# An attention-then-MLP kernel: the first rows of k are loaded in float32 by SyncE and rounded on chip

## The chip, the cores and the metric

The kernel runs on one core of one Trainium2 chip. The metric is the device time of one execution in microseconds (us), as the median of several runs; lower is better. Five engines work side by side and meet through semaphores: TensorE (PE, with its weight loads shown as PEld), VectorE (DVE), ScalarE (ACT), GpSimd (POOL) and SyncE (SP). Loads and stores are DMAs, which an engine issues from its own queue and which then run beside the engines.

## The reference

Two stages in a row, with float32 inputs and a float32 output:

- Attention over 8 batches, 8 heads, 576 positions and 64 channels a head. A query sees its own position and the 127 before it. Each head adds a linear bias: minus its slope (1/2, 1/4, ... 1/256) times the distance.
- The heads side by side make 4608 rows of 512. They go through `h = x @ w_in` (512 by 2048), an ELU, and `@ w_out` (2048 by 512).

```python
scores = scale * np.matmul(q, k.transpose(0, 1, 3, 2))
scores = np.where((rel >= 0) & (rel < 128), scores + bias[None], -1e9)
attn = softmax(scores);  x = attn @ v
h = x @ w_in
out = np.where(h > 0, h, np.exp(np.minimum(h, 0)) - 1) @ w_out
```

## The kernel before, in words

**Types and loads.** Everything on chip is float16, except sums and the output. The inputs are float32, so every load is a DMA issued by GpSimd, which converts on the way (L101 for the first two batches' q and k, L108 for later ones, L114 v, L119 w_in, L122 w_out). GpSimd issues them in the order of the code, one after another, between its other work. SyncE issues the stores of the output and the transposes of x of later batches; its first store is issued at 40.7 us.

**Batches 0 and 1** bring q and k with rows on partitions, and TensorE turns them by transposes (`turn_first`, L136) into PSUM. A copy by DVE or ACT (L140) then puts the turned pieces into `QT` and `KT`, with channels on partitions. `split` says how a batch's 576 rows are cut into parts: for part 0 of batch 0, 256 rows as 64 partitions with 4 rows each. So one half (four of eight heads) is 16 small transposes of 64x64. Later batches are turned by DVE (L145).

**Scores of batch 0** have the bias added by TensorE: `early_bias` (L183) multiplies `SI` (for each head an identity times the head's slope) by `RB` (the distances, with a large negative number outside the window), and `early_scores` (L191) adds q times k into the same PSUM bank. `early_expo` (L197, L200) is the exponential on ACT. From batch 1 on the exponential of the plain score is multiplied by a table `TAB` instead (`first_weigh`, `weigh`); `TAB[:, 0]` is made by eight exponentials on ACT (L464), `TAB[:, 1]` by two copies on DVE (L473, L474). `values` (L253 to L260) multiplies by v and divides on DVE, `turn` (L289, L290) turns the result into `xT`.

**The MLP** takes rows of `xT` as they come: `hidden` (L305) multiplies by w_in, ACT and GpSimd make the exponential side of the ELU into `e` (L312 to L316), `elu` (L323, DVE) puts both sides together into `g`, and `output` and `product` (L329, L393) multiply by w_out.

**The order** is written out by hand. What an engine gets first in the code it does first. The start (L428 to L488) is a plain list: a memset for the warming matmuls, GpSimd's loads and memsets, DVE's chain from the iota of positions (L432) through the identity (L454), the distances (L455 to L457) and `SI` (L460), ACT's eight exponentials, 22 matmuls on ones (`warm`, L424) that keep TensorE busy, then batch 0's first turns, biases, scores and values:

```python
load_first(0, 1, 0)                      # k, 256 rows
nc.gpsimd.iota(rel, pattern=[[1, 256]], base=0, channel_multiplier=-1)
load_first(0, 0, 0)                      # q, 256 rows
load_v(0, 0)
load_v(0, 1)
load_wi(0)
```

After it comes a plan of numbered slots, each with one step of `hidden`. `at(s, f, ...)` puts a piece of work into slot s; in a slot come first the pieces of `before`, then `hidden`, then the `elu` of the slot before (`done`; in slots 1, 4 and 5 it stands elsewhere), then the pieces of `at` in the order of the code, then outputs. In the profile slot 0 begins on TensorE at 13.01 us, slot 3 at 20.66, slot 4 at 22.42.

**Buffers the change touches.** `T` are four tiles of 128 x 2048 float16, filled with sums of w_out's blocks from slot 11 on; until then `fore[1]` to `fore[4]` are the same memory used for other things (`far`, `RB`, `SI`, `rel`, `wz`). `fore[2]` is not used early. `st` is a ring of two buffers for the q and k of batches from 2 on. `hp`, `op`, `av`, `sp` are PSUM banks.

Of the kernel before, what the change touches and what calls it, by code (L numbers as in the profile page):

```python
# [7 lines left out]
F32 = mybir.dt.float32  # L8
F16 = mybir.dt.float16
I32 = mybir.dt.int32  # L10
AF = mybir.ActivationFunctionType
# [7 lines left out]
def kernel(  # L19
# [9 lines left out]
    nc = tc.nc  # L29
    B, H, S, D = q.shape  # L30
# [6 lines left out]
    R = S // 64  # L37
    V = nc.vector

    const = ctx.enter_context(tc.tile_pool(name="const", bufs=1))  # L40
    stage = ctx.enter_context(tc.tile_pool(name="stage", bufs=2))
# [7 lines left out]
    def one(shape, dt, name):  # L49
        return const.tile(shape, dt, name=name, tag=name)  # L50
# [6 lines left out]
    fore = [t.rearrange("p j c -> p (j c)") if t is not None else None for t in T]  # L57
    RB = fore[3][:, 1024:1536]
# [3 lines left out]
    TAB = one([128, 2, 4, 2, 256], F16, "TAB")  # L62
# [14 lines left out]
    sp = [spa[:, 0, :], spa[:, 1, :]] + [ps_s.tile([128, 512], F32, name=f"sp{i}", tag=f"sp{i}") for i in (2, 3)]  # L77
    hp = [ps_h.tile([128, 512], F32, name=f"hp{i}", tag=f"hp{i}") for i in range(2)]
    av = ps_v.tile([128, 512], F32, name="av", tag="av")
    op = ps_o.tile([128, 512], F32, name="op", tag="op")  # L80
    AB = sp[0:2]
# [3 lines left out]
    st = {}  # L85
    s0 = gpool.tile([128, NFC * 512], F16, name="s0", tag="g")
    s1 = one([128, 2 * H * 6 * D], F16, "s1")
    s0 = [t[:, 0:2 * H * 6 * D].rearrange("p (w h j d) -> p w h j d", w=2, h=H, j=6) for t in (s0, s1)]

    def split(b, w, part):  # L90

        if b == 0 and w == 1:
            return ((0, 64, 4, 0, 0), (64, 64, 5, 256, 0))[part]
        if b == 0:
            return ((0, 64, 4, 0, 0), (64, 64, 2, 256, 0), (64, 64, 3, 384, 2))[part]
        return ((0, 128, 4, 0, 0), (0, 64, 1, 512, 4))[part]

    def load_first(b, w, part):

        p0, n, m, r0, j0 = split(b, w, part)  # L100
        nc.gpsimd.dma_start(  # L101
            s0[b][p0:p0 + n, w, :, j0:j0 + m, :].rearrange("p h j d -> p h (j d)"),
            (q, k)[w][b, :, r0:r0 + n * m, :].rearrange("h (p j) d -> p h (j d)", j=m))

    def load_qk(b, w, g):
        if b not in st:
            st[b] = stage.tile([128, 2, 2, R, 2, D], F16, name="st")
        nc.gpsimd.dma_start(  # L108
            st[b][32 * g:32 * g + 32, w, :, :, :, :].rearrange("p h n j d -> p (h n) (j d)"),
            (q, k)[w][b, 2 * g:2 * g + 2, :, :].rearrange("h (n i j) d -> i (h n) (j d)", i=32, j=2))  # L110
# [16 lines left out]
    def turn_first(b, w, part, half, bank, copy):  # L127

        p0, n, m, r0, j0 = split(b, w, part)
        nh = 4 if n * m < 256 else 2  # L130
        t = bank.bitcast(F16)[:, 0:nh * m * n].rearrange("p (x j r) -> p x j r", x=nh, j=m)
        r = slice(p0, p0 + n)
        for x in range(nh):
            for j in range(m):
                for hh in range(2):
                    nc.tensor.transpose(t[64 * hh:64 * hh + 64, x, j, :], s0[b][r, w, 4 * hh + nh * half + x, j0 + j, :],  # L136
                                        ident[r, r])
        t = t.rearrange("p x j r -> p x r j")
        o = (Q0, K0)[w][b][:, nh * half:nh * half + nh, r0:r0 + m * n]
        copy(o.rearrange("p x (r j) -> p x r j", j=m), t)  # L140
# [8 lines left out]
    with tc.manual_schedule():  # L149
# [29 lines left out]
        def early_bias(banks, c0):  # L179

            for x in range(4):
                for hh in range(2):
                    nc.tensor.matmul(banks[hh][:, 128 * x:128 * x + 128], SI[:, 4 * hh + x, :], RB[:, c0:c0 + 128],  # L183
                                     start=x == 0, stop=False, skip_group_check=True)

        def early_scores(banks, u, c0):
            k0, q0 = 128 * u, 128 * u + c0
            for x in range(4):
                for hh in range(2):
                    r = slice(64 * hh, 64 * hh + 64)  # L190
                    nc.tensor.matmul(banks[hh][:, 128 * x:128 * x + 128], kt_[0][r, x * S + k0:x * S + k0 + 128],  # L191
                                     Q0[0][r, x, q0:q0 + 128], start=False, stop=True, skip_group_check=True)
# [50 lines left out]
        def values(b, i, part, bank=av):  # L243

            m = 128 if i < 4 else 64
            banks = (part, part + 2) if b < 2 else (2 * part, 2 * part + 1)
            parts = [(3, 128, 3), (3, 192, 4)] if i == 4 else [(i, 0, i)] + ([(i - 1, 128, i - 1)] if i else [])
            a = bank[:, 0:4 * (D + 1)].rearrange("p (x h d) -> p x h d", x=2, h=2)
            for x, g in enumerate(banks):
                for h2 in range(2):  # L250
                    for j, (u, c, n) in enumerate(parts):
                        c += 512 * g + 256 * h2
                        nc.tensor.matmul(a[:, x, h2, :], ex_[u][:, c:c + 128], VP[b % 2][:, n, 2 * g + h2, 0:D + 1],  # L253
                                         start=j == 0, stop=j == len(parts) - 1)
            if part == 0:
                xnt[b, i] = work.tile([128, 4, 2, D], F16, name="xn", tag="xn", bufs=4)
            o = xnt[b, i][0:m, part::2, :, :] if b < 2 else xnt[b, i][0:m, 2 * part:2 * part + 2, :, :]
            r = work.tile([128, 2, 2], F32, name="rden", tag="rden", bufs=2)
            V.reciprocal(out=r[0:m], in_=a[0:m, :, :, D])
            V.tensor_tensor(out=o, in0=a[0:m, :, :, 0:D], in1=r[0:m].unsqueeze(3).broadcast_to([m, 2, 2, D]),  # L260
                            op=ALU.mult)
# [18 lines left out]
        def turn(b, i, copy=None, bank=op):  # L280
            n = 128 if i < 4 else 64
            o = (b * S + 128 * i) % RING
            x = xnt.pop((b, i)).rearrange("p g h d -> p (g h d)")
            if copy is None:
                nc.sync.dma_start_transpose(out=xT[:, :, o:o + n], in_=x[0:n, :])
                return
            t = bank.bitcast(F16)[:, 0:512].rearrange("p (c r) -> p c r", c=4)
            for c in range(4):
                nc.tensor.transpose(t[:, c, 0:n], x[0:n, 128 * c:128 * c + 128], ident[0:n, 0:n])  # L289
            copy(xT[:, :, o:o + n], t[:, :, 0:n])  # L290
# [131 lines left out]
        def warm(n, bank=op):  # L422
            for _ in range(n):
                nc.tensor.matmul(bank[:, 0:256], wz[:, 0:128], wz, start=True, stop=True)  # L424
# [3 lines left out]
        rel = fore[3][:, 1536:2048].bitcast(I32)  # L428
        far = fore[1][:, 0:256]
        V.memset(wz, 1.0)  # L430
        load_first(0, 1, 0)
        nc.gpsimd.iota(rel, pattern=[[1, 256]], base=0, channel_multiplier=-1)  # L432
        load_first(0, 0, 0)
        load_v(0, 0)
        load_v(0, 1)
        load_wi(0)
        load_first(0, 0, 1)
        load_first(0, 1, 1)
        load_first(0, 0, 2)
# [18 lines left out]
        slope = [2.0 ** (-8.0 * (h + 1) / H) for h in range(H)]  # L458
# [1 line left out]
            V.tensor_scalar(out=SI[:, h, :], in0=ident, scalar1=8.0 * slope[h], scalar2=None, op0=ALU.mult)  # L460
        V.memset(VP[0][:, :, :, D:D + 1], 1.0)

        for h in range(H):
            nc.scalar.activation(TAB[:, 0, h // 2, h % 2, :], RB[:, 0:256], AF.Exp, scale=slope[h])  # L464
        warm(22)
        turn_first(0, 1, 0, 0, hp[0], V.tensor_copy)
        turn_first(0, 1, 0, 1, op, V.tensor_copy)
        early_bias(AB, 0)
        turn_first(0, 0, 0, 0, hp[1], nc.scalar.copy)
        turn_first(0, 0, 0, 1, av, V.tensor_copy)  # L470
        V.tensor_copy(RB[:, 256:448], RB[:, 0:192])
        V.tensor_copy(RB[:, 448:512], RB[:, 0:64])
        V.tensor_copy(TAB[:, 1, :, :, 0:192], TAB[:, 0, :, :, 0:192])  # L473
        V.tensor_copy(TAB[:, 1, :, :, 192:256], TAB[:, 0, :, :, 0:64])  # L474
        early_bias(sp[2:4], 128)
        early_scores(AB, 0, 0)
        early_expo(AB, 0, 0)
        early_scores(sp[2:4], 0, 128)
# [5 lines left out]
        values(0, 0, 1, op)  # L484
        warm(5, sp[0])
        turn(0, 0, V.tensor_copy, hp[0])
        values(0, 1, 0)
        values(0, 1, 1, op)  # L488

# [3 lines left out]
        def at(s, f, *a):  # L493
            tasks.setdefault(s, []).append((f, a))
# [29 lines left out]
        for o in range(16 * NTB):  # L524
            t, ts, f = o // 16, o // 4 % 4, o % 4
# [32 lines left out]
        at(5, first_scores, 0, 3, 1, 0)  # L558
        at(5, first_expo, 0, 3, 1, 0, 0, 256)
        at(5, done, 4)  # L560
        at(9, values, 0, 3, 0)
        at(9, values, 0, 3, 1, sp[3])
        at(10, values, 0, 4, 0)
# [35 lines left out]
        for b in range(2, B):  # L599
            for u in range(4):  # L600
                a = START[b] + 4 * u
# [11 lines left out]
            a = START[b - 1] if b > 2 else 0  # L613
# [85 lines left out]
```

The softmax here doesn't subtract the row's maximum and nothing guards it: scores larger than these inputs give would overflow.

## Time and profile before

| | us |
|---|---|
| median of 3 runs | 311.22 |
| lowest and highest run | 310.29, 312.43 |
| span of the profiled execution | 308.9 |
| own time of the profiled execution | not listed |
| PE busy | 300.1 |
| DVE busy | 257.5 |
| ACT busy | 241.8 |
| POOL busy | 108.4 |

The span is the time from the first to the last instruction of the profiled execution; a run's time also has what lies around it. The own time of the profiled execution is not listed, only its span; the median of the three runs is 2.3 us over that span. The views used below give times from the start of the span. A timeline row is start, duration, engine, line, operation, output and inputs, shapes and count; in brackets stands how long the engine was idle before it and what ended that wait. A row with a count covers several instructions that follow each other. A row of waits is who waited for whom: total us, times, longest. A row of DMA issues gives the KB as written and the us from issue to landing. GpSimd's rows of DMAs are the issuing alone.

### The profile page before, as it was taken

Reading aid. Unit: us, or ns where it says so; the run is one execution under the profiler, and the core shown is the slowest. Engines: PE = TensorE matmul, PEld = TensorE weight load, DVE = VectorE, ACT = ScalarE, POOL = GpSimd, SP = SyncE. Lnnn points to the kernel's source line nnn. Section 1 sums busy time; section 2 is a strip of 40 time slices with the busy share of each in tenths; the row PEclk is TensorE's granted clock in tenths of the full one; section 3 lists DMA queues with packets and bytes.
Section 4 is the critical chain, followed back from the end, with each engine's and each line's share of the span. In section 5 each row is a group of like instructions: output and inputs, shape, how many; then the busy total and the mean of one; then the engine's idle time right before and its main releaser. Section 6 shows DMA issues by size and latency. Waiting matters only on the chain.

```text
span 308.9 us, 9820 instructions
## 1 busy us (share of the span) xinstructions
PE 300.1 (97%) x4071; PEld 256.1 (83%) x4071; DVE 257.5 (83%) x498; ACT 241.8 (78%) x446; POOL 108.4 (35%) x163
## 2 busy tenths in 40 slices
PE   6899999999999999999999999999999999999995
PEld 4788875798888888988888888888899888898884
DVE  4646888988989998997989998989998788886782
ACT  4576678678798788878887889778888897968871
POOL 8937867273252315141616061706000001010000
PEclk9999999999999999999999999999999999999999
DMA  9999999999194919395969896999530202030103
GB/s 96 196 197 202 201 180 185 94 118 115 21 165 63 169 35 161 43 152 59 132 70 138 110 102 78 138 124 122 60 94 7 91 17 87 19 98 0 70 28 110
DMA packets 96509, 32.04 MB, mean 104 GB/s; under 512 B 83920, under 2 KB 91984, under 8 KB 96464
## 3 DMA queue, kind: packets, MB, share of 16 engines
q0 software_dynamic: 75920, 18.36, 64.2%
q1 hardware_dynamic: 20400, 12.98, 17.1%
q8 instruction: 32, 0.52, 0.7%
q14 instruction: 13, 0.11, 0.1%
q10 hardware_dynamic: 144, 0.07, 0.1%
HBM read 36.70 MB, written 9.44 MB: 149 GB/s over the span
## 4 chain that ended last, share of the span: by engine, by line
PE 72%; DVE 8%; DMA 6%; ACT 5%; POOL 4%; issue 4%; POOLq 0%; DVEq 0%
PE hp L305 33%; PE op L393 13%; PE av L393 12%; DMA VP<-in_v_dram 4%; PE spa L225 3%; PE spa L271 3%; DVE g L323 3%; POOL e L316 2%; PE sp L393 2%; ACT e L315 2%; DMA s<-in_q_dram 2%; ACT EX L236 1%; PE sp L253 1%; POOL VP L114 1%; DVE xn L260 1%
## 5 line engine op out<-in xcount | busy, mean ns | idle before, releaser
L305 PE MATMUL hp<-xT,wi 128*128 128x256 f16 (+3 forms) x1488 | 144.2, 245 | 1.0 <-DVE g L323 0.5
L305 PEld LDWEIGHTS <-wi 128*128 128x128 f16 x1600 | 119.9, 98 | 18.1 <-issue 6.3
L323 DVE SCALAR_TENSOR_TENSOR g<-e,hp 128x512 f16<-128x512 f32 x138 | 93.7, 679 | 22.2 <-ACT e L313 12.5
L316 POOL TENSOR_SCALAR e<-e 128x512 f32<-128x512 f32 x44 | 28.0, 636 | 158.8 <-ACT e L315 152.9
L312 ACT ACTIVATE e<-hp 128x512 f32<-128x512 f32 x98 | 58.6, 597 | 28.5 <-PE hp L305 23.1
L313 ACT ACTIVATE e<-e 128x512 f32<-128x512 f32 x100 | 63.1, 631 | 3.2
L393 PEld LDWEIGHTS <-S 128*128 128x128 f16 x544 | 51.2, 98 | 6.7 <-issue 0.6
L393 PEld LDWEIGHTS <-g 128*128 128x128 f16 x408 | 38.2, 98 | 4.7 <-issue 0.6
L241 DVE TENSOR_TENSOR EX<-EX,TAB 128x1024 f16<-128x1024 f16 x48 | 32.9, 686 | 6.2 <-ACT EX L236 4.0
L114 POOL DMA_DIRECT2D VP<-in_v_dram x40 | 34.6, 878 | 0.6 <-PE hp L305 0.3
L315 ACT ACTIVATE e<-hp 128x512 f32<-128x512 f32 x40 | 24.1, 601 | 10.9 <-PE hp L305 10.9
L393 PE MATMUL op<-T,S 128*128 128x256 f16 x200 | 30.0, 273 | 0.1
L233 ACT ACTIVATE EX<-spa 128x1024 f16<-128x1024 f32 x24 | 24.6, 1025 | 3.7 <-PE spa L225 3.4
L393 PE MATMUL av<-T,S 128*128 128x256 f16 x176 | 26.4, 273 | 0.1
L236 ACT ACTIVATE EX<-sp 128x512 f16<-128x512 f32 x48 | 26.0, 596 | 0.0
L354 DVE TENSOR_TENSOR S<-g 128x1024 f16<-128x1024 f16 (+2 forms) x35 | 23.5, 671 | 0.8 <-PE op L393 0.2
L393 PE MATMUL op<-wo,g 128*128 128x256 f16 x128 | 19.2, 272 | 0.1
L393 PE MATMUL av<-wo,g 128*128 128x256 f16 x120 | 18.0, 272 | 0.0
L277 DVE TENSOR_TENSOR xn<-spa,rden 128x512 f16<-128x512 f32 x24 | 16.6, 692 | 0.8
L108 POOL DMA_DIRECT2D st<-in_k_dram x24 | 16.2, 686 | 2.8 <-DMA s<-in_q_dram 1.9
L108 POOL DMA_DIRECT2D st<-in_q_dram x24 | 15.9, 666 | 0.6 <-DMA VP<-in_v_dram 0.6
L271 PE MATMUL spa<-VP,EX 128*128 128x65 f16 x336 | 15.4, 193 | 0.1
(139 smaller groups left out, 379.3 us busy)
## 6 DMA issues: line engine op xcount, KB each, us to landing
out_dram<-ob SPq DMA_DIRECT2D x35, 256.0 KB, 2.2
VP<-in_v_dram POOLq DMA_DIRECT2D x32, 128.0 KB, 5.7
st<-in_k_dram POOLq DMA_DIRECT2D x24, 144.0 KB, 5.2
st<-in_q_dram POOLq DMA_DIRECT2D x24, 144.0 KB, 5.9
wi<-in_moe_w_in_dram POOLq DMA_DIRECT2D x4, 512.0 KB, 10.7
wo<-in_moe_w_out_dram POOLq DMA_DIRECT2D x4, 512.0 KB, 10.1
VP<-in_v_dram POOLq DMA_DIRECT2D x8, 64.0 KB, 5.8
s<-in_k_dram POOLq DMA_DIRECT2D x1, 512.0 KB, 12.1
```

Of the source, the lines that this page charges most:

```text
L108: nc.gpsimd.dma_start(st[b][32 * g:32 * g + 32, w, :, :, :, :].rearrange("p h n j d -> p (h n) (j d)"), (q, k)[w][b, 2 * g:2 * g + 2, :, : ...
L114: nc.gpsimd.dma_start(VP[b % 2][0:p, n, :, 0:D], v[b, :, 128 * n:128 * n + p, :].rearrange("h p d -> p h d"))
L236: nc.scalar.activation(unit(b, u)[:, g, :, :], sp[g].rearrange("p (h c) -> p h c", h=2), AF.Exp, scale=0.125)
L241: V.tensor_tensor(out=e, in0=e, in1=TAB[:, int(u == 3), 2 * gp:2 * gp + 2, :, :], op=ALU.mult)
L271: nc.tensor.matmul(a[:, h // 4, h % 4, :], ex_[u][:, c:c + 128], VP[b % 2][:, n, h, 0:D + 1], start=j == 0, stop=j == len(parts) - 1)
L305: nc.tensor.matmul(p[:, l * w + u0:l * w + u1], w_in_sb[:, c, fc * 128:(fc + 1) * 128], xT[:, c, x0:x0 + u1 - u0], start=(c == 0), stop=(c ...
L312: nc.scalar.activation(e[:, 0:n], p[:, 0:n], AF.Relu, scale=-1.0)
L313: nc.scalar.activation(e[:, 0:n], e[:, 0:n], AF.Exp, scale=-1.0)
L315: nc.scalar.activation(e[:, 0:n], p[:, 0:n], AF.Exp)
L316: nc.gpsimd.tensor_scalar(out=e[:, 0:n], in0=e[:, 0:n], scalar1=1.0, scalar2=0.0, op0=ALU.min, op1=ALU.max)
L323: V.scalar_tensor_tensor(out=gs[t][:, f0:f0 + nf, c0:c0 + w], in0=sh(es.pop((t, c0, f0))), scalar=1.0, in1=sh(hps.pop((t, c0, f0))), op0=A ...
L393: nc.tensor.matmul(o, a[:, j, :], b[:, j, :], start=j == 0 and i in (1, 2, 5), stop=j == 7, skip_group_check=True)
```

## The change

- Part 0 of batch 0's k (256 rows of all heads) is no longer loaded by GpSimd with conversion. `load_raw` issues four loads from SyncE's queue, in float32, into a buffer of `st`'s ring: two for each half (`half` 0 has heads 0, 1, 4, 5). `cook` copies each half into float16 in `fore[2]`: half 0 on DVE, half 1 on ACT. `turn_first` reads that place for this part.
- That part now lies as 128 partitions with 2 rows each, so a half is 8 transposes of 128x64.
- With k's load gone from GpSimd's queue, the iota is its first piece of work and the load of q its first load.
- TensorE: 18 warming matmuls for 22. Both sets of biases stand ahead: the first before any turn, the second between the two turns of k.
- The copies from the four turns: k's first half on DVE, its second on ACT, q's first on DVE, its second on ACT (before: DVE, DVE, ACT, DVE).
- ACT makes five exponentials of `TAB[:, 0]` at the start and the other three after the exponentials of batch 0's first scores, ahead of slot 0.
- DVE's two copies into `TAB[:, 1]` move from the start into slot 3, behind that slot's other pieces.

```diff
@@ -90,7 +90,7 @@
     def split(b, w, part):
 
         if b == 0 and w == 1:
-            return ((0, 64, 4, 0, 0), (64, 64, 5, 256, 0))[part]
+            return ((0, 128, 2, 0, 0), (64, 64, 5, 256, 0))[part]
         if b == 0:
             return ((0, 64, 4, 0, 0), (64, 64, 2, 256, 0), (64, 64, 3, 384, 2))[part]
         return ((0, 128, 4, 0, 0), (0, 64, 1, 512, 4))[part]
@@ -101,6 +101,21 @@
         nc.gpsimd.dma_start(
             s0[b][p0:p0 + n, w, :, j0:j0 + m, :].rearrange("p h j d -> p h (j d)"),
             (q, k)[w][b, :, r0:r0 + n * m, :].rearrange("h (p j) d -> p h (j d)", j=m))
+
+    raw = stage.tile([128, 2, 2, R, 2, D], F16, name="st")
+    raw = raw.rearrange("p a b n j d -> p (a b n j d)").bitcast(F32)[:, 0:1024].rearrange(
+        "p (a b x j d) -> p b a x (j d)", a=2, b=2, x=2, j=2)
+    cooked = fore[2][:, 0:1024].rearrange("p (h j d) -> p h j d", h=H, j=2)
+
+    def load_raw(half):
+
+        for a in range(2):
+            h = 4 * a + 2 * half
+            nc.sync.dma_start(raw[:, half, a], k[0, h:h + 2, 0:256, :].rearrange("x (p j) d -> p x (j d)", j=2))
+
+    def cook(half, copy):
+
+        copy(cooked.rearrange("p (a b x) j d -> p b a x (j d)", a=2, b=2)[:, half], raw[:, half])
 
     def load_qk(b, w, g):
         if b not in st:
@@ -130,10 +145,11 @@
         nh = 4 if n * m < 256 else 2
         t = bank.bitcast(F16)[:, 0:nh * m * n].rearrange("p (x j r) -> p x j r", x=nh, j=m)
         r = slice(p0, p0 + n)
+        src = cooked if (b, w, part) == (0, 1, 0) else s0[b][:, w]
         for x in range(nh):
             for j in range(m):
                 for hh in range(2):
-                    nc.tensor.transpose(t[64 * hh:64 * hh + 64, x, j, :], s0[b][r, w, 4 * hh + nh * half + x, j0 + j, :],
+                    nc.tensor.transpose(t[64 * hh:64 * hh + 64, x, j, :], src[r, 4 * hh + nh * half + x, j0 + j, :],
                                         ident[r, r])
         t = t.rearrange("p x j r -> p x r j")
         o = (Q0, K0)[w][b][:, nh * half:nh * half + nh, r0:r0 + m * n]
@@ -428,7 +444,8 @@
         rel = fore[3][:, 1536:2048].bitcast(I32)
         far = fore[1][:, 0:256]
         V.memset(wz, 1.0)
-        load_first(0, 1, 0)
+        for half in range(2):
+            load_raw(half)
         nc.gpsimd.iota(rel, pattern=[[1, 256]], base=0, channel_multiplier=-1)
         load_first(0, 0, 0)
         load_v(0, 0)
@@ -460,19 +477,22 @@
             V.tensor_scalar(out=SI[:, h, :], in0=ident, scalar1=8.0 * slope[h], scalar2=None, op0=ALU.mult)
         V.memset(VP[0][:, :, :, D:D + 1], 1.0)
 
-        for h in range(H):
-            nc.scalar.activation(TAB[:, 0, h // 2, h % 2, :], RB[:, 0:256], AF.Exp, scale=slope[h])
-        warm(22)
+        def table(h0, h1):
+            for h in range(h0, h1):
+                nc.scalar.activation(TAB[:, 0, h // 2, h % 2, :], RB[:, 0:256], AF.Exp, scale=slope[h])
+
+        table(0, 5)
+        warm(18)
+        cook(0, V.tensor_copy)
+        cook(1, nc.scalar.copy)
+        early_bias(AB, 0)
         turn_first(0, 1, 0, 0, hp[0], V.tensor_copy)
-        turn_first(0, 1, 0, 1, op, V.tensor_copy)
-        early_bias(AB, 0)
-        turn_first(0, 0, 0, 0, hp[1], nc.scalar.copy)
-        turn_first(0, 0, 0, 1, av, V.tensor_copy)
+        early_bias(sp[2:4], 128)
+        turn_first(0, 1, 0, 1, op, nc.scalar.copy)
+        turn_first(0, 0, 0, 0, hp[1], V.tensor_copy)
+        turn_first(0, 0, 0, 1, av, nc.scalar.copy)
         V.tensor_copy(RB[:, 256:448], RB[:, 0:192])
         V.tensor_copy(RB[:, 448:512], RB[:, 0:64])
-        V.tensor_copy(TAB[:, 1, :, :, 0:192], TAB[:, 0, :, :, 0:192])
-        V.tensor_copy(TAB[:, 1, :, :, 192:256], TAB[:, 0, :, :, 0:64])
-        early_bias(sp[2:4], 128)
         early_scores(AB, 0, 0)
         early_expo(AB, 0, 0)
         early_scores(sp[2:4], 0, 128)
@@ -484,6 +504,7 @@
         values(0, 0, 1, op)
         warm(5, sp[0])
         turn(0, 0, V.tensor_copy, hp[0])
+        table(5, H)
         values(0, 1, 0)
         values(0, 1, 1, op)
 
@@ -558,6 +579,8 @@
         at(5, first_scores, 0, 3, 1, 0)
         at(5, first_expo, 0, 3, 1, 0, 0, 256)
         at(5, done, 4)
+        at(3, V.tensor_copy, TAB[:, 1, :, :, 0:192], TAB[:, 0, :, :, 0:192])
+        at(3, V.tensor_copy, TAB[:, 1, :, :, 192:256], TAB[:, 0, :, :, 0:64])
         at(9, values, 0, 3, 0)
         at(9, values, 0, 3, 1, sp[3])
         at(10, values, 0, 4, 0)
```

## The prediction

> **What bounds the kernel now.** I read the busy shares first, then TensorE's own waits, then the start in the timeline, since every edit but one lies in the first 13 us.
>
> ```profile
> PE 300.1 (97%) x4071; PEld 256.1 (83%) x4071; DVE 257.5 (83%) x498; ACT 241.8 (78%) x446; POOL 108.4 (35%) x163
> ```
>
> TensorE is busy for 300.1 of 308.9 us, so 8.8 us are idle. The waits from 15 us to the end of the span name little of that:
>
> ```profile
> PE hp L305 <- DVE g L323: 0.5, 2, 0.3
> PE spa L176 <- ACT QT L140: 0.3, 1, 0.3
> ```
>
> Of named waits, 0.8 us remain after 15 us, and none is on a DMA. From there on TensorE runs one long list; if that list begins earlier, nothing that the profile shows gives the time back. The start has the long wait, in TensorE's timeline:
>
> ```profile
> 1.20 4.01 PE L424 MATMUL op<-T 128*128 128x256 f16 x22 [1.20 <-DVE T L430]
> 5.47 0.44 PE L136 MATMUL hp<-ident,s 64*64 64x64 f16 x16 [0.26 <-DMA s<-in_k_dram]
> 5.74 0.42 PE L136 MATMUL op<-ident,s 64*64 64x64 f16 x16
> 6.09 0.62 PE L183 MATMUL spa<-T 128*128 128x128 f16 x8
> 7.68 0.44 PE L136 MATMUL hp<-ident,s 64*64 64x64 f16 x16 [0.97 <-DMA s<-in_q_dram]
> ```
>
> TensorE turns k at 5.47, does one set of biases and stands until q lands at 7.63. The chain of waits agrees: GpSimd issues k, builds its table of positions, issues q, and then a DMA is the chain.
>
> ```profile
> 1.25 0.84 POOL s L101
> ...
> 2.18 0.29 POOL T L432
> 2.47 5.16 DMA s<-in_q_dram
> 7.63 0.04 issue
> 7.68 0.44 PE hp L136 x16
> ```
>
> So the arrival of q sets the start, and q goes out behind k's issue and the iota.
>
> **The change, part by part.**
>
> *q's issue.* k's issue (0.84 us) leaves GpSimd's queue and the iota comes first. Both shift to the front: the queue's first instruction starts at 1.25, the iota to q's issue took 2.47 - 2.18 = 0.29, so q issues at about 1.54 instead of 2.47.
>
> *q's landing.* The issues between 1 and 3 us give two prices:
>
> ```profile
> s<-in_k_dram POOLq DMA_DIRECT2D x1, 256.0 KB, 4.2
> s<-in_q_dram POOLq DMA_DIRECT2D x1, 256.0 KB, 5.2
> ```
>
> 4.2 us is a load with nothing in front of it, 5.2 one with 256 KB in front of it in the same queue. q now leads its queue, but raw k (8 heads x 256 rows x 64 x 4 bytes = 512 KB as written) runs beside it. That gives 5.74 to 6.74; I take 4.7, the middle, so 6.2. If q had to wait for all of k after all, the price is 4.2 plus the 2.2 between the two landings (5.4 and 7.6): 7.9, the far end.
>
> *Raw k.* No load by SyncE is in the trace; its stores are the nearest rows. Quiet ones landed in 2.0 us (220 to 232 us), those beside GpSimd's loads in 5.7 (40 to 50 us), each 256 KB. An issue takes 0.33 us there for 128 rows of 2 KB; four issues with 256 pieces each take 0.33 to 0.66. The other engines begin at 0.74 to 0.87, so the first half is issued by 1.5 and the second by 2.7 at the latest. Between 1.2 and 2 us the DMA view shows no packet at all, and k's first came at 2.75, 1.5 us after its issue; q's would come near 3.1. SyncE's transfers therefore start on idle engines, and I take the quiet price: halves landed at 3.5 and 4.7 (contested: 7.2 and 8.4).
>
> A rule of the Trainium skill speaks against the split: "DMA: Bandwidth & Descriptors", section "Issuing engines are not separate DMA queues", says that DMAs from several engines run on the same 16 DMA engines and that a second issuer saves issue time only. By it alone q would land at the far end, 7.9, and the sum would be no gain; the empty DMA view before 2.75 us is why I do not use it.
>
> *Rounding.* Two copies of 128x512 from float32 to float16. For ACT the row is `e<-hp`, 0.60 us. For DVE no such copy is shown; between the 128x256 TENSOR_SCALAR (0.23) and the 128x512 SCALAR_TENSOR_TENSOR (0.68) I take 0.6. DVE's chain from the iota ended at 4.87 and shifts by 0.93 to 3.94, so half 0 is rounded at 4.54. ACT's tables began at 3.90, now 2.97; five of eight take 5/8 of 2.56 = 1.6, so 4.6; half 1 lands at 4.7 and is rounded at 5.3.
>
> DVE's copies can also stand beside GpSimd's issues: the 192-column copy L471 took 0.50. That may hold half 0 to 5.2 or so, which is still near its turn.
>
> The page "SBUF — State Buffer", section "SBUF: two separate sides", warns that a float32 copy on DVE inside SBUF keeps GpSimd from writing DMA descriptors. By it v's issue would slip by the 0.6 of one copy; no row here shows such a copy.
>
> *TensorE's order.* Four of the 22 warming matmuls go, the last ones, 0.11 each (five later ones took 0.71, one alone 0.27): they end at 4.77, the next can start at 4.65. Then biases 0.5, eight transposes of half k, biases 0.5, eight transposes. Batch 1 has this 128x64 form: 16 from 42.62 to 43.09, so 0.23 for eight. TensorE is ready for q at 4.65 + 0.5 + 0.23 + 0.5 + 0.23 = 6.1. Each rounded half is there 0.4 us or more before its turn; beyond that a late half delays everything one for one. q at 6.2 is the later one: q's transposes start at 6.25 instead of 7.68, **1.43 earlier** (1.58 if q is there by 6.1; 0.9 if it lands at 6.74; -0.3 if at 7.9).
>
> *From q to the first exponential.* Before: 7.68 to 9.48 = 1.80, its last step DVE's copy of the second half of q, 8.41 + 0.69. Now ACT copies that half in 0.58: 0.1 less. The biases that stood behind q's transposes now stand before them, where TensorE waited anyway; they also hid nothing but that copy. **0.1 earlier** (0 to 0.2).
>
> *Three exponentials of the table later on ACT.* 3 x 0.31 = 0.96, in front of the first `e`; ACT idled 1.63 us there (12.47 to 14.10). Nothing, with 0.6 to spare. RB's copies sit where TensorE works on its scores: nothing.
>
> *TAB's two copies, moved to slot 3 on DVE.* They took 9.22 to 10.51 = 1.29 where DVE was free. In slot 3:
>
> ```profile
> 22.20 0.69 DVE L323 SCALAR_TENSOR_TENSOR g<-e,av 128x512 f16<-128x512 f32 x1 [2.44 <-POOL e L316]
> 23.77 0.18 DVE L259 RECIPROCAL rden<-av 128x4 f32<-128x4 f32 x1 [0.88 <-PE av L253]
> ```
>
> There DVE has 0.88 us until `rden`. 1.29 does not fit: `rden`, both `xn` and TensorE's transposes of `xn` (25.02, weight load waiting on DVE) come up to 0.41 later, and TensorE behind them. If the copies are quicker there, nothing. **0.2 later** (0 to 0.41).
>
> *What is late next.* wi's first quarter landed at 5.16 + 6.7 = 11.85; its reader starts at 13.01: slack 1.16 against a shift of 1.5. Its queue has lost k ahead of it and begins no later, so I expect it 0.5 to 1 us sooner. If not, 0.35 of the gain is lost. Quarters two and three (landed 18.0 and 20.9, read at 19.76 and 22.42) have 1.8 and 1.5.
>
> *Sum.* -1.43 - 0.1 + 0.2 = -1.3 us. The profiled span of 308.9 becomes 307.6. The median, 311.22, is 2.3 above that span (time around it, and other executions, which spread from 310.29 to 312.43); I leave those 2.3 as they are: **309.9**.
>
> **The rivals.**
>
> *q is hidden behind k after all* (chance 0.20). For it: the engines are full from about 4 us on, and the far end of q's landing, 7.9. Against it: the idle DMA engines before 2.75. It gives +0.3 - 0.1 + 0.2 = +0.4, so 311.6; where q is only half as late, 310.8.
>
> *Raw k takes q's place as the wait* (0.12), the one that ends slower. Its place is the second half of raw k, the fourth issue on SyncE. At the contested price it lands at 1.8 + 5.7 = 7.5 to 8.4; rounding 0.6 and eight transposes 0.23 follow, and q's turn stands behind them: 8.3 to 9.2 instead of 7.68, 0.6 to 1.5 later. With 0.2 to 0.4 of slot 3: 312.0 to 313.1. It decides from a landing past 7.68 - 0.23 - 0.6 = 6.85. For it: 5.7 in the only stores that ran beside GpSimd's loads. Against it: those queues were full for 30 us before, this one is empty.
>
> *The gain is made and not kept* (0.14): wi waits 0.35, slot 3 costs 0.41, q lands at 6.74: -0.9 - 0.1 + 0.4, and wi no longer matters: 310.6.
>
> **How the numbers follow.** My forecast (0.54) reaches from 1.58 + 0.2 gained and no cost (309.4) to 310.4, and the medians here differ by about 0.7 us either way with nothing changed. So 308.7 at the low end; the high end takes in the kept-in-part case and hidden q: 311.9, leaving out most of raw k's 0.12 and the noise beyond both ends. About 1% (3.1 us) is what a measurement of this kernel can tell from no change. All gains together are 1.8 and all losses 1.9, so both outer classes need something not priced here: 0.04 each.
>
> **What would show it.** q's issue near 1.5 and its landing near 6.2; the raw halves rounded before 5.1 and 5.7; TensorE's q transposes at 6.25, first scores near 7.4, first exponential near 7.9, `hp L305` near 11.5 without a wait on wi; TAB's copies after `g` in slot 3 with `rden` up to 0.4 late against its neighbours. I am wrong if q still lands after 7.5, if TensorE waits on a rounding copy, or if the 1.5 us are there at 13 us and gone at 60.

## The result and the profile after

The changed kernel is slower by 0.4%. Its median is 311.99 us against 310.99 us for the kernel before, 17 executions each; the ratio is 1.004 with a 95% interval of 1.0023 to 1.0058. Forecast were 309.9, from 308.7 to 311.9: the measured time lies just above the upper end. Two later executions of before, of 377 and 604 us, were disturbed as a whole and are counted nowhere below.

The profiled execution took 311.12 us, with a span of 309.3 against 308.9. In the executions of both kernels whose span is listed, 1.7 to 2.0 us lie around it, in the median 1.8, so part of the comparison can be made in spans. First the busy shares of the changed kernel (engine, busy us, share, instructions):

```profile
PE 299.7 (97%) x4051; PEld 255.9 (83%) x4051; DVE 257.8 (83%) x498; ACT 243.0 (79%) x448; POOL 107.7 (35%) x162
```

TensorE has 20 instructions less and the same busy time to 0.4 us. The difference is in when its list starts. TensorE's timeline at the start (start, duration, what, and in brackets how long it was idle and who ended that):

```profile
4.79 0.61 PE L199 MATMUL spa<-T 128*128 128x128 f16 x8
5.33 0.41 PE L152 MATMUL hp<-ident,T 128*64 128x128 f16 x8
5.68 0.62 PE L199 MATMUL sp<-T 128*128 128x128 f16 x8
7.64 0.41 PE L152 MATMUL op<-ident,T 128*64 128x128 f16 x8 [1.34 <-ACT T L118]
7.98 0.44 PE L152 MATMUL hp<-ident,s 64*64 64x64 f16 x16
```

The order is the one written in the change, and the first steps come 0.1 to 0.3 behind the forecast (4.65, 5.15 and 5.38 for the first three rows). Then TensorE stands 1.34 us, and not for q: it waits for ACT's rounding of k's second half (L118). q's turn follows at 7.98 without any wait of its own, 0.30 later than before's 7.68. The chain of waits of the same kernel says who held the rounding (start, duration, link):

```profile
1.76 0.46 SPq L114
2.22 0.04 issue
2.27 4.62 DMA st<-in_k_dram
6.88 0.02 issue
6.91 0.02 ACTq L118
6.92 0.04 issue
6.97 0.63 ACT T L118
7.59 0.04 issue
7.64 0.41 PE op L152 x8
8.05 0.39 PE hp L152 x16
```

q has left the chain. In its place stands the last of SyncE's four loads of raw k, 4.62 us from its issue. The four were issued at 0.74, 1.26, 1.76 and 2.27 and landed at 2.90, 4.04, 6.63 and 6.88; the third and the fourth are the second half. q's load (issues of GpSimd between 1.3 and 2 us: KB, us to landing):

```profile
s<-in_q_dram POOLq DMA_DIRECT2D x1, 256.0 KB, 5.3
```

q was issued at 1.35 and landed at 6.61, one microsecond before the 7.63 of before, and 0.27 before the raw half that TensorE turns first.

The moved copies of TAB, in DVE's timeline in slot 3 of the changed kernel:

```profile
22.38 0.69 DVE L339 SCALAR_TENSOR_TENSOR g<-e,av 128x512 f16<-128x512 f32 x1 [2.44 <-POOL e L332]
22.99 1.17 DVE L687 COPY TAB<-TAB 128x1536 f16<-128x1536 f16 x2
24.08 0.17 DVE L275 RECIPROCAL rden<-av 128x4 f32<-128x4 f32 x1
```

`rden` has no idle time before it any more: it starts 0.31 later than before (23.77), of which 0.19 came in from the start. The waits of TensorE from 15 us to the end:

```profile
PE hp L321 <- DVE g L339: 0.5, 2, 0.3
PE spa L192 <- ACT QT L156: 0.3, 1, 0.3
PE sp L305 <- DVE xn L276: 0.2, 1, 0.2
```

The third line is new and follows from those copies. If each weight load of TensorE is set against the same one of before, counted from the end of the list, the changed kernel is 0.19 later at 13 us, 0.29 later from 26 us on, and still 0.29 later at 285 us. The last 0.16 of the 0.45 between the spans come behind the last matmul; their cause was not looked for.

So one pair of traces accounts for some 0.3 us of TensorE's list; the medians differ by 1.0. The rest of this text looks for both parts.

### The profile page after: what moved, and what is told of

The parts are those of the page before. It is cut to its first block, busy times and chain, and to the rows that moved or that the text cites. A ratio compares the mean times of both kernels' runs of the same rounds, so it can differ in the third digit from the quotient of the medians.

```text
span 309.3 us, 9795 instructions
## 1 busy us (share of the span) xinstructions
PE 299.7 (97%) x4051; PEld 255.9 (83%) x4051; DVE 257.8 (83%) x498; ACT 243.0 (79%) x448; POOL 107.7 (35%) x162
## 4 chain that ended last, share of the span: by engine, by line
PE 75%; DVE 9%; ACT 7%; issue 4%; POOL 2%; DMA 1%; SPq 0%; DVEq 0%; POOLq 0%; ACTq 0%
PE hp L321 34%; PE op L409 13%; PE av L409 12%; PE spa L241 3%; PE spa L287 3%; DVE g L339 3%; PE sp L409 2%; POOL e L332 2%; ACT e L331 2%; ACT EX L252 2%; DMA st<-in_k_dram 1%; PE op L345 1%; PE sp L269 1%; ACT e L328 1%; DVE S L370 1%
```

## The experiments

Two theories were put to the test. **The late half**: raw k's second half lands late because q's load runs beside it, and it stands ahead of q in TensorE's order. **The clock**: the waits that the change puts behind the warming matmuls let TensorE's granted clock fall in some executions. The mean granted clock of an execution tells: in the traces taken at 0.997 or above it did not fall before the last matmul, and the two at 0.993 have 3.41 us at half rate in the first 13 us. Beside the experiments before had 7 of 114 executions under 0.997; the changed kernel had 8 of 17 with the result and 2 of 8 later.

| kernel | ratio to before, 95% | first exponential, us | list at 26 us against before's trace | median span of executions at 0.997 or above | below 0.997 |
|---|---|---|---|---|---|
| before | | 9.48 | 0 | 308.55 to 309.0 by set | 7 of 114 |
| the change | 1.0040 [1.0023, 1.0058] | 9.68 | +0.29 | 309.4 | 8 of 17 |
| ctl | 1.0004 [0.9988, 1.0020] | 8.94 | +0.06 | 309.2 | 0 of 12 |
| fill | 1.0032 [1.0019, 1.0045] | 9.87 | +0.48 | 310.0 | 0 of 11 |
| qfirst | 1.0011 [0.9994, 1.0027] | 9.18 | -0.20 | 308.9 | 1 of 10 |
| halfraw | 0.9983 [0.9966, 0.9999] | 8.25 | -1.14 | 308.4 | 0 of 10 |
| aft | 1.0031 [1.0017, 1.0045] | 10.03 | +1.34 | 309.45 | 2 of 8 |
| delay | 1.0025 [1.0008, 1.0042] | 8.97 | +0.12 | 309.1 | 3 of 12 |
| best | 1.0037 [1.0022, 1.0053] | 10.05 | +1.25 | 309.55 | 2 of 12 |
| tab6 | one execution | 9.79 | +0.31 | 309.4 | 0 of 1 |
| qtab | 1.0000 [0.9986, 1.0014] | 9.67 | +0.18 | 309.05 | 0 of 12 |
| qtabfill | 1.0024 [1.0006, 1.0041] | 9.88 | +0.39 | 309.5 | 2 of 12 |
| split | 1.0037 [1.0014, 1.0059] | 8.30 | +2.04 | 309.4 | 4 of 12 |
| noraw | 1.0018 [0.9989, 1.0046] | 8.69 | +1.87 | 309.05 | 2 of 12 |

The third and fourth columns are of one profiled execution each; those of aft, best, split and noraw hold a stretch at half clock. Each ratio is to executions of before taken in the same set; the count of before includes ctl, and the clocks of the 17 of before that belong to the result are not listed.

### The kernel before once more (ctl)

No edit: how far does one execution of the same program stand from the next?

> The kernel before once more, unchanged, to see the granted clock of each of its executions. Clock theory: the changed kernel's executions spread from 0.989 to 1.0 in mean granted clock and its longest ones are those of the low clocks; if that is the change's doing, the unchanged kernel keeps 0.998 or more in nearly all executions and stays within 310 to 311.5 us. Rival (the spread has nothing to do with the change): the unchanged kernel shows 0.989 to 0.995 about as often, 7 of 17 or so. The ratio to the kernel before should be 1.000.

Measured: the medians agree (311.01 and 311.0), and none of 12 executions is below 0.997 (the longest took 312.09). But its trace is not the trace that the prediction worked from. q landed at 7.09 and not at 7.63, the first exponential came at 8.94, and TensorE was 0.54 earlier at 11 us. At 13 us that was gone. The waits of TensorE in the first 30 us of this execution:

```profile
PE sp L136 <- DMA s<-in_q_dram: 0.5, 1, 0.5
PE hp L305 <- DMA wi<-in_moe_w_in_dram: 0.4, 1, 0.4
PE hp L305 <- DVE g L323: 0.3, 1, 0.3
```

wi's first quarter, issued at 4.95, landed at 12.97 and held the first hidden matmuls (13.02 against 13.01). In the trace of before q's last part was late by itself: of the 16 engines' parts of that load fifteen had landed by 6.99 and one at 7.63. So two things follow. The start is a row of gates (q, wi's first quarter, then the next parts of q and k), each set by its last engine, which differs from execution to execution; and what an early q gives is kept only if wi is early too.

### The second half of raw k not loaded (halfraw)

```diff
-        for half in range(2):
-            load_raw(half)
+        load_raw(0)
 def cook(half, copy):
-    copy(..., raw[:, half])
+    copy(..., raw[:, 0])
```

> The changed kernel without SyncE's loads of the second half of raw k; both roundings read the first half instead, so heads 2, 3, 6 and 7 of batch 0's first rows get other heads' k and that part of the result is not the reference's. All instructions but two loads are there. Late-half theory: no rounding waits, TensorE is ready for q near 6.1, q has 256 KB instead of 512 KB beside it and lands near 5.8, so the first exponential is near 7.9 and the span about 307.7: the gain that was forecast. Rival (q lands near 6.6 whatever runs beside it, because its own queue is slow to start): q's turn at 6.6, first exponential near 8.4, span about 308.1.

The timelines of ACT and of TensorE in this kernel:

```profile
4.51 0.62 ACT L118 CAST T<-st 128x512 f16<-128x512 f32 x1 [0.17 <-DMA st<-in_k_dram]
8.25 1.02 ACT L213 ACTIVATE EX<-spa 128x1024 f16<-128x1024 f32 x1 [0.38 <-PE spa L207]
```

```profile
6.21 0.41 PE L152 MATMUL op<-ident,T 128*64 128x128 f16 x8
6.55 0.44 PE L152 MATMUL hp<-ident,s 64*64 64x64 f16 x16
```

With 256 KB less in SyncE's queue the same order runs without a wait: the rounding begins at 4.51 and not at 6.97, q (landed 5.98) is turned at 6.55 and not at 7.98, the first exponential comes 1.43 earlier than with the change. This is the prediction's start, 0.3 late (6.25 and 7.9 were forecast). It shows that the two loads of the second half are what keeps the gain away, by their own lateness and by what they cost q (5.98 for 6.61), which this kernel does not tell apart. It also shows how little the gain is: the list is 1.14 ahead in this execution, but this was the shortest of ten spans (307.7 to 308.8), and the ratio is 0.9983, some 0.5 us.

### q ahead of k's second half (qfirst)

```diff
-        turn_first(0, 1, 0, 1, op, nc.scalar.copy)
         turn_first(0, 0, 0, 0, hp[1], V.tensor_copy)
         turn_first(0, 0, 0, 1, av, nc.scalar.copy)
+        turn_first(0, 1, 0, 1, op, nc.scalar.copy)
```

> The changed kernel with q's two turns moved ahead of the turn of k's second half on TensorE (and ACT's copies in that order). Late-half theory: q, landed at 6.6, is turned at about 6.7 in the time in which TensorE idled, only k's second half waits for its rounding at 7.6, its copy ends near 8.7 and the first exponential starts near 9.2 instead of 9.68: the profiled span falls by 0.4 to 0.5 us, to about 308.9. Rival (q's own landing or ACT's copies set the start, not the second half of k): no change of the first exponential, 9.6 to 9.7.

TensorE's timeline:

```profile
6.74 0.44 PE L152 MATMUL hp<-ident,s 64*64 64x64 f16 x16 [0.29 <-DMA s<-in_q_dram]
7.01 0.42 PE L152 MATMUL av<-ident,s 64*64 64x64 f16 x16
7.75 0.41 PE L152 MATMUL op<-ident,T 128*64 128x128 f16 x8 [0.32 <-ACT T L118]
8.10 0.28 PE L207 MATMUL spa<-QT,KT 64*128 64x128 f16 x4
```

q landed at 6.70 and is turned at once; the half that landed at 7.00 is late for a shorter stretch. The first exponential comes at 9.18, 0.5 before the change's. No difference from before is left that can be told (interval 0.9994 to 1.0027). The place of the late half in TensorE's order is thus worth about 0.5 us at the first exponential; its lateness remains.

### Fillers behind the second biases (fill)

```diff
         early_bias(sp[2:4], 128)
+        warm(12, op)
         turn_first(0, 1, 0, 1, op, nc.scalar.copy)
```

> The changed kernel with 12 more warming matmuls on TensorE in the stretch where it idles from 6.3 to 7.6 us, between the second set of biases and the turn of k's second half; 12 x 0.11 = 1.3 us, so nothing should start later. Clock theory (the idle stretch and the four warming matmuls that were taken away let the granted clock fall in some executions): all executions at 0.998 or more, median down by 0.7 us from 312.0 to about 311.3, the profiled span still 309.3. Rival (late rounding alone is the loss, the clock is chance): the clocks keep their spread and the median stays near 312.0.

Twelve warming matmuls keep TensorE busy where the change leaves it idle. None of 11 executions fell below 0.997. The median of 311.76 is still 0.76 above before: the full-clock span is 310.0, longer than the change's. In the trace q's turn starts at 8.17 and not at 7.98, since TensorE reached the half at 7.83 and not at 7.64. The clock stayed up, as the clock theory has it, but at a price that took most of it back: 311.76 where 311.3 was expected.

### The change once more (aft)

> The changed kernel once more, unchanged, beside the others on one chip, for its granted clocks. Clock theory: some four or five of ten executions below 0.997, these at 312 to 314 us; the others at 310.9 to 312.2 with a median near 311.2, which is 0.2 to 0.3 over the kernel before, as the late start and slot 3 give it. Rival (the low clocks of the changed kernel were chance or another chip): as rare as in the kernel before, 3 of 34, and a median near 311.3.

It repeats the result: 1.0031. Two of its 8 executions are below 0.997, where some four or five of ten were expected, and one of 24 of before beside it. At full clock alone it is still 0.9 us over before in this set (spans of 309.45 and 308.55). Its profiled execution is one with a fallen clock. Three stretches of 3.41 us (busy time of each engine with its instructions in brackets, granted clock, DMA share, GB/s):

```profile
core 0: us, PE busy (x) PEld busy (x) DVE busy (x) ACT busy (x) POOL busy (x), PEclk, DMA share, GB/s
5.92:9.33 3.41, 2.07 (x58) 1.63 (x57) 1.38 (x3) 1.64 (x3) 3.37 (x6) 1.00 1.82 186
9.33:12.74 3.41, 3.36 (x43) 2.64 (x43) 0.87 (x4) 2.86 (x6) 3.24 (x11) 0.50 1.41 196
12.75:16.16 3.41, 3.06 (x60) 2.47 (x58) 2.40 (x9) 1.81 (x5) 0.90 (x2) 1.00 1.36 203
```

From 9.33 to 12.74 the granted clock is 0.50: 43 matmuls take 3.36 us. The list is 1.34 later than before's at 26 us, 1.05 more than in the undisturbed trace of the same program. This stretch follows one in which TensorE was busy for 2.07 of 3.41 us. Over both sets the change's executions at full clock have a median of 311.2, those below 0.997 one of 312.7.

### q's load held back (delay)

```diff
+        nc.gpsimd.memset(VP[0][64:128, 4, :, 0:D], 0.0)
+        nc.gpsimd.memset(kt_[0][:, 4 * S:4 * S + 128], 0.0)
         load_first(0, 0, 0)
```

The two memsets are moved from a later place, so that q is issued at 1.96 and not at 1.35.

> The changed kernel with two of GpSimd's later memsets (0.52 and 0.20 us) put ahead of its load of q, so that q issues near 2.1 instead of 1.35. Theory (SyncE's loads nearly stop for the first microsecond of GpSimd's queue, 14 to 34 KB a us against 200 to 270 before it): raw k's second half is through before q's first packet at about 3.7 and lands near 4.3 instead of 6.9; no rounding waits; q lands near 6.4; first exponential near 8.2; span near 307.8; clocks at 0.998 or more; median 309.9. Rival (the raw loads are slow by themselves, four issues of 256 pieces): the second half still lands after 6 and q later than before, 7.2 or so; span 309.5 or more.

SyncE's third load landed at 4.48 and not at 6.63: that part agrees with the theory that q's start is what stops SyncE's queue. The fourth landed at 6.12, fifteen of its 16 parts by 5.73, where about 4.3 was expected; q landed at 7.24. Holding q back costs q what it gives k, wi is issued 0.7 later as well, and the ratio is 1.0025. In the trace the list is 0.51 ahead at 13 us and 0.05 behind at 18, after the next parts of k and q, which landed at 16.66 and 17.56 (fifteen of the 16 parts by 14.75 and 16.15). The expected gain did not come.

How the two queues share, in the DMA view of the changed kernel (queue, packets, MB, share of the engines), first from 2.25 to 3 us, then from 3.25 to 4.25; q1 is SyncE's queue, q0 GpSimd's:

```profile
q1 hardware_dynamic: 344, 0.16, 73.7%
q0 software_dynamic: 2, 0.00, 1.2%
```

```profile
q0 software_dynamic: 128, 0.07, 69.4%
q1 hardware_dynamic: 46, 0.02, 10.5%
```

Alone, SyncE's queue moved 0.16 MB in 0.75 us. Once q's packets come it moves 0.02 MB in a whole microsecond, while q0 itself moves only 0.07 MB as written. With q held back the same view, from 3.25 to 3.75 us, has:

```profile
q1 hardware_dynamic: 182, 0.09, 59.3%
```

There q0 has not begun, and SyncE's queue moves 0.09 MB in half a microsecond, nearly its pace from before (0.18 against 0.21 MB a us).

### TAB's copies in slot 6 (tab6, best)

```diff
-        at(3, V.tensor_copy, TAB[:, 1, :, :, 0:192], ...)
-        at(3, V.tensor_copy, TAB[:, 1, :, :, 192:256], ...)
+        at(6, V.tensor_copy, TAB[:, 1, :, :, 0:192], ...)
+        at(6, V.tensor_copy, TAB[:, 1, :, :, 192:256], ...)
```

> The changed kernel with DVE's two copies into TAB in slot 6 instead of slot 3. Theory: up to slot 4 TensorE is 0.2 us behind the kernel before, as in the changed kernel; the further 0.1 us that the changed kernel loses at slot 4 to 5 is not lost, so TensorE's step at 44 us is 0.2 instead of 0.29 behind. Rival (the 0.1 us comes from something else in slot 4): 0.29 again.

The list is 0.31 late at 13 us (the half landed at 7.00 here) and 0.31 late at 26 and at 285: the step of 0.10 in slot 3 is gone. One execution, and a small thing, but the trace shows the place.

> The kernel with q's load behind the two memsets, and DVE's two copies into TAB in slot 6 instead of slot 3, behind the last `g` before DVE's 1.3 us of idling. Theory: as with the memsets alone, and 0.1 us more (the copies cost nothing in slot 6): span near 307.7, median 309.8, faster than both kernels. Rival (the raw loads are slow by themselves): 309.4 or more.

This is delay and tab6 together. It does not beat before: 1.0037. In its trace fifteen of the 16 parts of the fourth load were there by 5.17 and the last at 7.04; q had fifteen by 7.44 and the last at 8.14; and the clock fell from 9.06 to 12.47.

### Both orders together, with and without fillers (qtab, qtabfill)

qtab is qfirst and tab6 together; qtabfill adds `warm(3, op)` ahead of q's turns and ahead of k's second half.

> The changed kernel with both mends that showed a gain: q turned ahead of k's second half, and DVE's copies into TAB in slot 6. Theory (the two losses are separate and add): TensorE 0.3 us ahead of the kernel before at 13 us and still 0.3 ahead at 44 us (q's order alone: 0.30 and 0.20), span near 308.7, median 0.3 below the kernel before. Rival (slot 6 costs what slot 3 cost): 0.2 ahead at 44 us.

> As that, with three warming matmuls ahead of q's turns and three ahead of the turn of k's second half, where TensorE idled 0.3 us each. Clock theory: no execution below 0.997, where the same kernel without them may still have one in ten; span the same within 0.1; median no higher. Rival: the fillers come in the way and cost 0.2 us or more, as the twelve did.

qtab equals before: 1.0000 [0.9986, 1.0014], none of 12 below 0.997. It is the best complete form of the change that was tried, 0.3 to 0.4% under the change as made, and no faster than before, where a gain of 0.3 us was expected. Its TensorE timeline has the row

```profile
7.37 0.44 PE L152 MATMUL hp<-ident,s 64*64 64x64 f16 x16 [1.40 <-DMA s<-in_q_dram]
```

with q's last part at 7.33 and the fifteen others by 6.49. TensorE idles 1.40 us here, as long as with the change, and the clock fell in no execution. qtabfill puts fillers there, is slower (1.0024), and has 2 of 12 below 0.997. So idle time behind the warming matmuls does not by itself decide: one execution had 1.40 us of it and kept its clock, and with fillers two fell. Over all sets it is not refuted as a part of the cause: 10 of 25 executions of the change fell, against 1 of 22 in qfirst and qtab, where q is turned in that time, 0 of 10 in halfraw and 0 of 11 in fill. The clock theory stays open.

### Half the raw load given back to GpSimd (split)

```diff
-        for half in range(2):
-            load_raw(half)
+        load_raw(0)
         nc.gpsimd.iota(...)
         load_first(0, 0, 0)
+        for h in (2, 6):
+            nc.gpsimd.dma_start(cooked[:, h:h + 2]..., k[0, h:h + 2, 0:256, :]...)
-        cook(1, nc.scalar.copy)
```

with q's turns first and TAB's copies in slot 6, as in qtab.

> Half 0 of k by SyncE in float32 as in the changed kernel; half 1 by GpSimd with conversion, straight into its place behind q, so that q has 256 KB of raw k beside it instead of 512 and half 1 needs no rounding; q turned ahead of half 1; DVE's copies into TAB in slot 6. Theory (the loads of raw half 1 are what holds back q and themselves): q lands near 6.0 as it did with half of raw k left out, half 1 near 6.9 (the price of the 128 KB behind q there), first exponential near 8.3, TensorE 0.9 ahead at 13 us; w_in's first quarter is then the next wait, so 0.7 to 0.9 ahead at 44 us; median 0.7 to 0.9 below the kernel before. Rival (half 1 in GpSimd's queue is late itself, 7.6 or more, as its engines straggle): 0.3 ahead or less.

q landed at 5.67 and the converted half at 6.83, so the start is good (8.30). Then TensorE waits again:

```profile
PE hp L321 <- DMA wi<-in_moe_w_in_dram: 2.1, 1, 2.1
```

Two more issues stand ahead of wi's on GpSimd, which goes out at 5.39 and not at 3.94; fourteen of its 16 parts landed by 11.85, the last at 14.05. The list is 2.04 late, a stretch at half clock after that wait included, and the median is 0.4% over before's, where 0.7 to 0.9 us of gain were expected.

### The other edits without raw k (noraw)

k's first 256 rows are GpSimd's first load again, on 64 partitions as in before; all other edits stay.

```diff
-        for half in range(2):
-            load_raw(half)
+        load_first(0, 1, 0)
-        cook(0, V.tensor_copy)
-        cook(1, nc.scalar.copy)
```

> The changed kernel with k's load given back to GpSimd as its first, before the iota, and no raw loads and no rounding; everything else of the change stays: 18 warming matmuls, both sets of biases ahead, shared copies, three exponentials of the table later, DVE's copies into TAB in slot 3. Theory (the raw loads beside q are the loss; the rest is worth -0.1 for the copies and +0.1 for slot 3): q lands near 7.6 as in the kernel before, first exponential near 9.4 (9.48 before, 9.68 in the changed kernel), TensorE 0.1 ahead at 13 us and even at 44 us, ratio to the kernel before 1.000. Rival (the moved edits carry a good part of the loss): 0.1 us or more behind at 44 us and a ratio of 1.002 or more.

q landed at 6.95 (near 7.6 was expected) and the first exponential came at 8.69, 0.25 before ctl's with q 0.14 earlier: in one execution of each, the shared copies and the biases ahead give the 0.1 that was forecast for them. Then, from TensorE's waits:

```profile
PE hp L318 <- DMA wi<-in_moe_w_in_dram: 1.5, 1, 1.5
```

wi, issued at 4.95, landed at 13.77, fourteen parts by 12.61. The ratio of 1.0018 with its interval from 0.9989 to 1.0046 shows no gain from the edits apart from raw k. At full clock its median span is 0.4 over before's in the same set (309.05 and 308.65), and the two lists of spans overlap. So the rival, that the moved edits carry a good part of the loss, is not excluded, and how much of the change's loss is due to raw k stays open.

## Why the prediction was wrong

**The step that failed** is raw k's landing: "SyncE's transfers therefore start on idle engines, and I take the quiet price: halves landed at 3.5 and 4.7". The engines were idle, and the first half landed at 4.04, 0.5 late. But the second half's packets were still to come when q's began near 3 us, and from then on its two loads took 4.87 and 4.62 from issue to landing. The contested row (5.7) was the nearer one; the quiet one (2.0) held for the first load alone (2.16; the second took 2.77). The working looked at what the engines were doing when the loads were issued, and not at what would arrive before the last of them was through.

**The rival "Raw k takes q's place as the wait"** came true, at its own threshold: it was to decide from a landing past 6.85, and the landing was 6.88. It was priced at 0.6 to 1.5, for a landing between 7.5 and 8.4; at the threshold it cost 0.30, since 1.10 us lie between the landing and q's turn (6.88 to 7.98) and not the 0.83 of rounding and eight transposes. That its 312.0 to 313.1 begin where the median lies (311.99) is luck: its wait made 0.30 of it, the clock and what was not found the rest. It had 0.12, against 0.54 for the forecast.

**The skill's rule on queues.** The prediction set the Trainium skill's "DMA: Bandwidth & Descriptors", section "Issuing engines are not separate DMA queues", aside. Measured, the loads did share the engines, as that section says. But the greater loss fell on SyncE's loads (0.02 MB in a microsecond). q lost less: 5.26 from issue to landing, against 4.63 in halfraw; it landed at 6.61, far from the 7.9 that the prediction worked out from the rule.

**q's issue and landing.** 1.35 for 1.54, and 6.61 for 6.2, within bounds of 5.74 to 6.74: right within its bounds, though from issue to landing it took 5.26 where 4.7 was priced, and the earlier issue hid 0.2 of that.

**TensorE's order.** Forecast ready for q at 6.1. In halfraw, with no wait left, it came to q at 6.55: the warming ended 0.14 later, and each set of eight transposes took 0.34 or 0.35 from start to start of the next where the row of sixteen in batch 1 had given 0.23 for eight. So the gain at q's turn, with raw k on time, is 1.13 and not 1.43.

**The baseline.** "Instead of 7.68" was one execution with a late last part; ctl had 7.13. Even with raw k on time, the gain at q's turn against that execution is 0.58 (7.13 - 6.55). That all of it would be kept was too much as well: halfraw, with the list 1.14 ahead in its trace, gained 0.5 in the median.

**What is late next.** wi was named, with a slack of 1.16 and an earlier issue. In the change it was issued at 3.94, landed at 11.06 and held nothing: right. But the slack was that of one trace. wi's first quarter landed between 11.06 and 14.05 in the traces of this study, and in ctl it took back a whole 0.54.

**From q to the first exponential.** 7.98 to 9.68 is 1.70, before it was 1.80: the 0.1 is there. The three late exponentials of the table cost nothing: ACT still idles 0.73 ahead of the first `e` (they took 1.05; the prediction's 3 x 0.31 is 0.93, and its 0.96 goes by the 0.32 of eight in 2.56). TAB's copies cost 0.10 in slot 3 (forecast 0.2, bounds 0 and 0.41); tab6 takes it away. v's two issues took 1.78 (2.03 before) and wi's, with DVE's rounding of half 0 in the middle of it, 0.92 (0.76). Of the 0.6 that the prediction worked out from the Trainium skill's page "SBUF — State Buffer", section "SBUF: two separate sides", at most 0.16 is to be seen. In aft, where the same issue took 0.77, it was the rounding that took longer, 0.78 for 0.43.

**What the list keeps.** "If that list begins earlier, nothing that the profile shows gives the time back": the same holds with the sign turned, +0.29 at 26 us is +0.29 at 285.

**What was not priced.** The list's 0.29 and the 0.16 at the end make 0.45 of the 1.0 us. In executions at full clock the change's span has a median of 309.4 against 308.55 to 309.0 of before, so 0.4 to 0.9; in aft, the one set with the clocks of both kernels, it is 0.9, and half of that is located in no trace. The rest goes with the granted clock: 10 of 25 executions of the change below 0.997 against 7 of 114, the change's own 1.4 us longer in the median than its others (312.7 against 311.2). With 8 of 17 such executions the falls make 0.8 of the result's median (311.99, and 311.2 without them), with 2 of 8 in aft 0.1. That the falls are more frequent is shown; what in the change brings them is not.

**The time around the span.** The prediction kept 2.3 us for it, from the median of three runs. It is 1.8, and before's median with more runs is 310.4 to 311.0; with 1.8 the same sum would have read 309.4. So the 2.3 brought the forecast nearer to the result by luck.

## What to carry to other kernels

When a load is given to a second queue so that two can run at once, price it by what runs beside its last packet, not by what the engines do at its issue, and order the reader so that the load that may be late is read last: that order alone was worth 0.2 to 0.3% here (1.0011 against 1.0031 and 1.0040). Before a wait of one trace is taken as the gain, look at the 16 parts of the load it waits for; one late part can be the luck of that execution, and the next gate (here wi's first quarter) gives back whatever it cannot follow.

## What the runs showed of the hardware

**A fall of the granted clock after a part of an idle stretch.** In aft, best, split and noraw the clock is 0.50 for one stretch of 3.41 us, behind a stretch of the same length in which TensorE was busy for 2.07, 2.26, 1.26 and 1.61 us. The Trainium skill's "TensorE: Matmul & The Clock Gate", section "Part 1: The HAM clock gate (the "warmup" mystery)", gives half rate after at least one idle window of about 3.4 us. The length agrees with the 3.41 seen here; a wholly idle stretch was not needed. Nor does the busy share alone decide: the first stretches of 3.41 us recorded at full clock were 2.07 busy in the trace of the change and 2.28 in that of before, and the clock stayed. What else decides is open.

**A queue that starts slowly and nearly stops the other.** In all these traces GpSimd's queue moved little in the first microsecond from its first packet: 0.04 to 0.08 MB as written, 0.06 in before, where no load by SyncE runs beside it. With the change, between 3.25 and 4.25 us, it moved 0.07 MB while the engines were counted 69% busy with it, and SyncE's queue fell to 0.02 MB in that stretch. Where the time of those first packets goes was not tried.

**The last of sixteen.** The same load, issued at the same time in the same code, landed at 6.5 to 7.3 (q), because one engine's part came up to 0.84 after the fifteen others. wi's first quarter took 6.7 to 8.8 us from issue to landing over the kernels. A late last part hit loads of both queues (in best SyncE's fourth load, fifteen parts by 5.17 and the last at 7.04).
